# Set-up of an FFT mixing and ReGLU kernel: constant rows in the angle products, rows of x in fewer transfers, weights asked for in another order, batch 1 loaded behind a token and its mirror gathered

## The chip, the cores and the metric

The kernel runs on one core of a Trainium2 chip, in one launch. The core has TensorE (matrix products, accumulating in eight PSUM banks), VectorE, ScalarE, GpSimd and SyncE (SP), each with an instruction queue of its own that is worked off in order; DMAs are issued from the queues of SP, ScalarE and GpSimd. The metric is device time in microseconds (us), the median of the runs shown.

## The reference

x has 8 batches of 3008 rows with 256 channels, in float32. Its two-dimensional Fourier transform over rows and channels is taken, the real part kept, and each of the 24064 rows goes through a ReGLU layer with 1536 hidden units:

```python
X = np.fft.fft(x, axis=1)
X = np.fft.fft(X, axis=2)
a = X.real.astype(np.float32).reshape(8 * 3008, 256)
gate = np.maximum(a @ w_gate, 0.0)
val = a @ w_val
out = (gate * val @ w_out).astype(np.float32)
```

## The kernel before, in words

The transform over channels is folded into the weights: WA and WB are cosine and sine tables (TA, TB) times w_gate (index 0) or w_val (index 1), WM is WB scaled. The transform over rows is a product with cosine and sine tables (tabC, tabS) on folded rows. A real transform has mirror symmetry, so each batch is folded first: XD holds rows upward (`load_rows`, L91), XG the same rows mirrored, and their sums and differences, halved twice more over rows and channels, are kept as F and G in bfloat16, in three parts t of 128, 128 and 120 or 121 partitions. Row 0 of both halves has a place of its own (partition 120 of part 2). From F and G the DFT steps make U (cosine part) and V (sine part); CB is a row for channel 128, made by the nyquist step (L620) from FN, written to DRAM (`keep_nyquist`, L630) and read back on all partitions (`row_128`, L993).

Then for each of 12 slices of the hidden units a gate (U times WA plus V times WB, L774 and L775) and, by adding WM (L779), the gate of the mirrored rows; the same for the value; ScalarE's relu (L789), VectorE's product (L798), later in one step (L809). h times wo (L692) gives the output rows, evicted by ScalarE and stored from SP.

Order is written out by hand; each engine works in program order and only data dependencies are added. The stages:

- **Set-up** (0 to 21 us). GpSimd makes index vectors (`iota`, L216). TensorE spins on zeros (`spin`, L263). An angle product (`angle`, L301) is three matmuls into one bank: row index times column index (`urow`, `krow`, L304), plus a constant 3008 x 1024 (`stride`, `offset`, L305), minus 3008 times a rounded quotient (L306); ScalarE takes its sine and cosine into the odd half of the tables. `turn` (L337) reverses part 0 of the mirror on TensorE with a permutation matrix; parts 1 and 2 of the mirror are gathered with indirect DMAs from GpSimd's queue (`load_mirror`, L108). VectorE folds batch 0 (L392 to L410). `hold` (L105) writes one element per half of XD on GpSimd, so that the row load behind it, which covers these elements, waits until GpSimd has come that far: a token. `load_w` (L286) and L361 load the weights from GpSimd's queue. `dft_first` (L530) then makes the first U and V, for the odd columns, together with the first weights (`combine`, L555).
- **Even part of batch 0**, on GpSimd: L414 to L423 (behind `go`, which VectorE writes when its fold is done), then `even_turns` (L438).
- **Batch 1's rows** are asked for at L462 to L466. The mirror takes two steps: `reverse` (L126) copies rows in reversed order from DRAM to DRAM (xr), `reverse_0` (L132) puts row 0 into its place there, `load_reversed` (L136) brings XG in. All are on SP's queue.
- **Batch 0 in four blocks** of 376 or 377 columns, 12 tiles each. Block 0 uses `first_tile` (L856), which also carries the remaining weights and the even tables as extra steps; blocks 1 to 3 use `single_tile` (L839). `fold_steps(1)` (L174) is emitted at the start of block 2 and `fold_steps(2)` at the start of block 3, on GpSimd, each with the row loads of the next batch; the DFT steps of batch 1 follow the tiles of blocks 2 and 3, as many per tile as `DFT_0` (L743) says: row 0 of that table is for block 1, row 1 for block 2, row 2 for block 3. The 25 steps are the nyquist step, then 24 products; the CB load goes with product 6, row 0 of V (L996) with product 21.
- **Batches 1 to 7** run in a software pipeline (`slot`, L918) over blocks of 512, 512 and 481 columns.

Of the kernel before, what the change touches and what calls it, by code (L numbers as in the profile page):

```python
# [33 lines left out]
def kernel(  # L34
# [50 lines left out]
    nc.vector.memset(FN[:], 0.0)  # L85
# [5 lines left out]
    def load_rows(b, ts=range(3), queue=None):  # L91
        o = b * S * D
        for t in ts:
            for r in range(2):
                n = (128, 128, 120)[t]
                (queue if queue and r else nc.sync).dma_start(out=XD[0:n, r, t],
                                                              in_=dram(x, o + (1 + r * H + t * 256) * D, [[2 * D, n], [D, 2], [1, D]]))
            if t == 2:
                for r in range(2):
                    if b == 0:  # L100
                        nc.sync.dma_start(out=XD[121:128, r, t],
                                          in_=dram(x, o + (1 + r * H + t * 256 + 2 * 121) * D, [[2 * D, 7], [D, 2], [1, D]]))
                    nc.sync.dma_start(out=XD[120:121, r, 2], in_=dram(x, o + r * H * D, [[0, 1], [0, 2], [1, D]]))

    def hold(t):  # L105
        nc.gpsimd.memset(XD[0:1, :, t, 0, 0:1], 0.0)
# [6 lines left out]

    def load_mirror_0(b):
        for r in range(2):
            nc.sync.dma_start(out=XG[120:121, r, 2, :, :].rearrange("p a d -> p (a d)"),
                              in_=dram(x, b * S * D + r * H * D, [[0, 1], [1, 2 * D]]))
# [56 lines left out]
    def fold_steps(b):  # L174
# [13 lines left out]
        for t in range(3):  # L188
            for i in range(2):
                steps.append((1.1, lambda i=i, t=t: fold_pq(e, p, i, t)))  # L190
                if (t, i) == (1, 0) and b + 1 < B:
                    steps.append((0.0, lambda: load_rows(b + 1)))
# [19 lines left out]
    load_rows(0, (0,), nc.scalar)  # L212
    load_rows(0, (1,))

# [27 lines left out]
    urow = single("urow", [1, 6, 128], F16, pool=st_)  # L242
    krow = single("krow", [1, NJ], F16, pool=st_)
    stride = single("stride", [1, 128], F16, pool=st_)
    offset = single("offset", [1, NJ], F16, pool=st_)
# [10 lines left out]

    warm = single("warm", [128, 512], BF16, pool=st_)
    nc.vector.memset(warm[:], 0.0)
    nc.vector.memset(half_pi[:], PI / 2)
    nc.vector.memset(stride[:], float(S))  # L260
# [811 lines left out]
```

## Time and profile before

| what | us |
|---|---|
| runs | 645.42, 645.14, 639.0 |
| median of the runs | 645.14 |
| the profiled execution's own time | 638.55 |
| its span, first to last instruction | 636.8 |
| TensorE busy in the span | 624.5 |
| VectorE, ScalarE, GpSimd busy | 553.6, 449.7, 495.3 |

The profile is one execution. Busy time of TensorE counts matmuls in the pipeline, so it says that work was under way, not that TensorE ran at its peak. A line of a timeline has the start, the duration, the engine, the line of the kernel, the operation, the tiles written and read, the shapes, how many instructions were merged, and in brackets the idle time before it and what ended it. L96 is line 96 of the kernel.

More rows of the same execution that matter here, from its timeline and its waits:

| what | start, us | note |
|---|---|---|
| first gate of block 0 (L774) | 20.99 | the next matmul (L775) at 21.86 |
| GpSimd: fold of the even part (L419 to L423) | 17.98 | third part ends at 29.42 |
| GpSimd: even turns | 30.07 | end at 38.00 |
| wo asked for (L361) | 15.30 | 23.9 us to landing |
| first use of wo (L692) | 39.24 | |
| SP: reverse of batch 1 (L130) | 18.40 | issued by 21.00 |
| SP: reverse_0 of batch 1 (L134) | 33.31 | 8.00 for both, with the waits |
| SP: load_reversed of batch 1 (L139) | 41.54 | |
| the nyquist step (L620) | 74.44 | |

### The profile page before, as it was taken

The numbers are of one execution on the slowest core, as the hardware profiler recorded it, in microseconds if no ns is written. First come the engines' busy times: TensorE is split into PE (matmuls) and PEld (weight loads), VectorE is DVE, ScalarE is ACT, GpSimd is POOL, SyncE is SP. The second block draws the span as 40 slices with busy tenths as digits, with TensorE's granted clock in tenths as the row PEclk, the third lists the DMA queues.
The fourth block names the chain that finished last, engine by engine and source line by source line (L and its number), as shares of the span: only waits on it lengthen the run. The fifth ranks groups of instructions, "written<-read, shape, count | busy, mean of one in ns | idle before, by whom it ended". The sixth has DMA issues, their size and how long they took to land.

```text
span 636.8 us, 12502 instructions
## 1 busy us (share of the span) xinstructions
PE 624.5 (98%) x4105; PEld 400.1 (63%) x4152; DVE 553.6 (87%) x983; ACT 449.7 (71%) x813; POOL 495.3 (78%) x479
## 2 busy tenths in 40 slices
PE   9999999999999999999999999999999999999997
PEld 2456676566666666666666666666666666666666
DVE  8797566998999999988999899899899989999991
ACT  6786666777777677777777777777777777777752
POOL 8837683899899999798888989799896666666660
PEclk9999999999999999999999999999999999999999
DMA  8955845724273426414272424321211111211122
GB/s 253 227 129 166 208 155 156 179 85 147 65 180 110 140 75 145 146 45 141 62 201 91 139 69 105 81 59 43 76 51 47 43 59 54 55 38 51 52 58 84
DMA packets 65523, 67.96 MB, mean 107 GB/s; under 512 B 20067, under 2 KB 47267, under 8 KB 65458
## 3 DMA queue, kind: packets, MB, share of 16 engines
q1 hardware_dynamic: 61522, 63.14, 34.4%
q0 software_dynamic: 3504, 3.38, 2.9%
q8 instruction: 32, 0.52, 0.4%
q10 hardware_dynamic: 432, 0.66, 0.3%
q14 instruction: 33, 0.27, 0.1%
HBM read 43.41 MB, written 35.70 MB: 124 GB/s over the span
## 4 chain that ended last, share of the span: by engine, by line
PE 85%; DVE 5%; POOL 3%; DMA 3%; issue 2%; SPq 1%; ACT 1%; DVEq 0%; ACTq 0%; POOLq 0%
PE o L692 35%; PE v L775 10%; PE v L779 9%; PE g L904 8%; PE p L911 8%; PE v L774 7%; PE d L503 4%; DVE h L809 3%; DMA XD<-in_x_dram 1%; DMA XG<-in_x_dram,gidx 1%; DMA CB<-ch 1%; PE p L779 1%; DVE r L915 1%; PE d L620 1%; DVE h L798 1%
## 5 line engine op out<-in xcount | busy, mean ns | idle before, releaser
L916 POOL TENSOR_TENSOR r<-r 128x512 f32<-128x512 f32 (+1 forms) x252 | 314.6, 1253 | 98.1 <-DVE r L915 97.7
L809 DVE SCALAR_TENSOR_TENSOR h<-r,v 128x512 bf16<-128x512 f32 (+1 forms) x504 | 318.6, 674 | 40.0 <-PE v L779 27.2
L692 PE MATMUL o<-wo,h 128*128 128x256 bf16 x2172 | 329.5, 272 | 0.0
L692 PEld LDWEIGHTS <-h 128*128 128x128 bf16 x2220 | 216.9, 98 | 112.3 <-issue 2.1
L899 ACT ACTIVATE p<-CB,b 128x512 f32<-128x512 bf16 (+1 forms) x252 | 172.4, 684 | 73.8 <-DVE r L915 72.5
L907 ACT COPY r<-g 128x512 f32<-128x512 f32 (+1 forms) x252 | 145.6, 578 | 66.6 <-PE g L904 58.9
L915 DVE SCALAR_TENSOR_TENSOR r<-r,p 128x512 f32<-128x512 f32 (+1 forms) x252 | 169.0, 671 | 0.8 <-ACT r L907 0.8
L779 PE MATMUL v<-V,WM 128*128 128x512 bf16 (+3 forms) x296 | 108.5, 367 | 2.8 <-DVE h L809 1.6
L775 PE MATMUL v<-V,WB 128*128 128x512 bf16 (+3 forms) x296 | 108.6, 367 | 2.3
L904 PE MATMUL g<-V,WM 128*128 128x512 bf16 (+1 forms) x252 | 94.5, 375 | 0.4 <-ACT r L907 0.3
L911 PE MATMUL p<-U,WA 128*128 128x512 bf16 (+1 forms) x252 | 94.5, 375 | 0.0
L774 PE MATMUL v<-U,WA 128*128 128x512 bf16 (+3 forms) x252 | 91.9, 365 | 0.3 <-DVE h L798 0.3
L148 POOL TENSOR_TENSOR XG<-XG,XD 128x510 f32<-128x510 f32 x42 | 53.3, 1280 | 21.7 <-issue 14.2
L798 DVE TENSOR_TENSOR h<-r,v 128x376 bf16<-128x376 f32 (+1 forms) x88 | 44.7, 543 | 19.4 <-PE v L779 12.4
L774 PEld LDWEIGHTS <-WA 128*128 128x128 bf16 x348 | 33.9, 98 | 42.7 <-issue 13.9
L703 ACT COPY os<-o 128x512 f32<-128x512 f32 x92 | 52.6, 572 | 4.7 <-issue 4.5
L775 PEld LDWEIGHTS <-WB 128*128 128x128 bf16 x348 | 33.9, 98 | 34.7 <-issue 0.7
L789 ACT ACTIVATE r<-p 128x376 f32<-128x376 f32 (+1 forms) x80 | 38.5, 487 | 19.5 <-PE p L779 10.7
L156 POOL TENSOR_TENSOR AA<-XG 128x510 f32<-128x510 f32 x42 | 45.4, 1091 | 0.0
L779 PEld LDWEIGHTS <-WM 128*128 128x128 bf16 x348 | 34.0, 98 | 7.8 <-ACT WM L593 0.5
L904 PEld LDWEIGHTS <-WM 128*128 128x128 bf16 x252 | 24.7, 98 | 6.4 <-issue 1.0
L911 PEld LDWEIGHTS <-WA 128*128 128x128 bf16 x252 | 24.6, 98 | 3.4 <-issue 0.5
(174 smaller groups left out, 390.6 us busy)
## 6 DMA issues: line engine op xcount, KB each, us to landing
out_dram<-os SPq DMA_DIRECT2D x124, 128.0 KB
xr<-in_x_dram SPq DMA_DIRECT2D x14, 768.0 KB
XG<-xr SPq DMA_DIRECT2D x14, 768.0 KB
XD<-in_x_dram SPq DMA_DIRECT2D x31, 256.0 KB
out_dram<-os SPq DMA_DIRECT2D x35, 112.0 KB
XD<-in_x_dram SPq DMA_DIRECT2D x16, 240.0 KB
CB<-ch SPq DMA_DIRECT2D x7, 376.2 KB
out_dram<-os SPq DMA_DIRECT2D x13, 96.0 KB
```

The costliest lines, as they stand in the source:

```text
L148: e.tensor_tensor(XG[p, r, t, ::-1, 1:D], XG[p, r, t, ::-1, 1:D], XD[p, r, t, :, D - 1:0:-1], op=ALU.add)
L692: nc.tensor.matmul(st["p"][0:m, q, :], lhsT=lhs(f), rhs=wo[:, f, :], start=(f == 0), stop=(f == NF - 1))
L774: nc.tensor.matmul(bank[:, 0:st["n"]], lhsT=WA[i][:, st["f"]], rhs=st["us"], start=True, stop=False)
L775: nc.tensor.matmul(bank[:, 0:st["n"]], lhsT=WB[i][:, st["f"]], rhs=st["vs"], start=False, stop=True)
L779: nc.tensor.matmul(bank[:, 0:st["n"]], lhsT=WM[i][:, st["f"]], rhs=st["vs"], start=False, stop=True, skip_group_check=True)
L809: nc.vector.scalar_tensor_tensor(half_h(st, sign), in0=st["s"][1 + sign][:, 0:n], scalar=0.0, in1=st["v"][:, 0:n], op0=ALU.max, op1=ALU.mult)
L899: nc.scalar.activation(st["p"][:, 0:st["n"]], st["c"], ACTF.Copy, scale=b2[:, st["fi"]:st["fi"] + 1])
L904: nc.tensor.matmul(st["g"][:, 0:n], lhsT=WM[0][:, st["f"]], rhs=st["vs"], start=True, stop=True)
L907: nc.scalar.copy(q[:, 0:n], st["g"][:, 0:n])
L911: nc.tensor.matmul(st["p"][:, 0:n], lhsT=WA[0][:, st["f"]], rhs=st["us"], start=False, stop=True, skip_group_check=True)
L915: nc.vector.scalar_tensor_tensor(sp[:, 0:n], in0=q[:, 0:n], scalar=-0.5, in1=st["p"][:, 0:n], op0=ALU.mult, op1=ALU.add)
L916: nc.gpsimd.tensor_tensor(sm[:, 0:n], sp[:, 0:n], q[:, 0:n], op=ALU.add)
```

## The change

Five parts:

1. **Angle products.** `stride` and `offset` are dropped with their matmul. `urow` and `krow` get 95 partitions: partition 0 holds the indices as before, the other 94 are constant, 256 in one and 128 in the other, and 94 x 256 x 128 is 3008 x 1024. The constants are written as pairs of float16 through a float32 view. The memset of FN moves from the first instruction of VectorE to behind four quotients. One `spin` between the second angle and the first turn is dropped.
2. **Rows.** `load_rows` takes both halves in one DMA per part (three instead of six); row 0 and seven spare rows have functions of their own, issued early for batch 0. The first part of batch 0 still goes in two halves, from SP and ScalarE.
3. **Weights.** The first load of w_val moves ahead of the sign table and the products with it on GpSimd. In the first tile, the first weight step is placed between the two matmuls of the gate.
4. **Batch 1.** `hold` on all three parts, behind `go`, lets batch 1's rows start only then. `reverse(1)`, `reverse_0(1)` and `load_reversed(1)` are dropped; six gathers from GpSimd's queue, behind the even turns, bring the mirror. The mirror's row 0 is loaded from SP, ahead of `reverse(2)`.
5. **DFT steps of batch 1.** In block 2 they begin with tile 2 instead of tile 6, and in block 3 there are at most two per tile but for one of three.

```diff
-    def load_rows(b, ts=range(3), queue=None):
-        o = b * S * D
+    def load_rows(b, ts=range(3)):
         for t in ts:
-            for r in range(2):
-                n = (128, 128, 120)[t]
-                (queue if queue and r else nc.sync).dma_start(out=XD[0:n, r, t],
-                                                              in_=dram(x, o + (1 + r * H + t * 256) * D, [[2 * D, n], [D, 2], [1, D]]))
...
+            n = (128, 128, 120)[t]
+            nc.sync.dma_start(out=XD[0:n, :, t].rearrange("p r a d -> p r (a d)"),
+                              in_=dram(x, (b * S + 1 + t * 256) * D, [[2 * D, n], [H * D, 2], [1, 2 * D]]))
+
+    def load_row_0(b):
+        for r in range(2):
+            nc.sync.dma_start(out=XD[120:121, r, 2], in_=dram(x, (b * S + r * H) * D, [[0, 1], [0, 2], [1, D]]))
+
+    def load_mirror_0(b):
+        nc.sync.dma_start(out=XG[120:121, :, 2, :, :].rearrange("p r a d -> p r (a d)"), in_=dram(x, b * S * D, [[H * D, 2], [1, 2 * D]]))
+
+    def load_spare():
+        for X in (XD, XG):
+            nc.sync.dma_start(out=X[121:128, :, 2, :, :].rearrange("p r a d -> p r (a d)"),
+                              in_=dram(x, 512 * D, [[2 * D, 7], [H * D, 2], [1, 2 * D]]))
...
-    def hold(t):
-        nc.gpsimd.memset(XD[0:1, :, t, 0, 0:1], 0.0)
+    def hold(ts):
+        nc.gpsimd.memset(XD[0:1, :, ts, 0, 0:1], 0.0)
...
-    load_rows(0, (0,), nc.scalar)
+    for r in range(2):
+        load_half(0, r, (nc.sync, nc.scalar)[r])
     load_rows(0, (1,))
+    load_row_0(0)
+    load_mirror_0(0)
+    load_spare()
...
-    urow = single("urow", [1, 6, 128], F16, pool=st_)
-    krow = single("krow", [1, NJ], F16, pool=st_)
-    stride = single("stride", [1, 128], F16, pool=st_)
-    offset = single("offset", [1, NJ], F16, pool=st_)
+    KA, UC, KC = 95, 256.0, 128.0
+    urow = single("urow", [KA, 6, 128], F16, pool=st_)
+    krow = single("krow", [KA, NJ], F16, pool=st_)
...
     nc.vector.memset(warm[:], 0.0)
+    nc.vector.memset(krow[:].bitcast(F32), pair_of(KC))
+    nc.vector.memset(urow[:].rearrange("p c k -> p (c k)").bitcast(F32), pair_of(UC))
     nc.vector.memset(half_pi[:], PI / 2)
-    nc.vector.memset(stride[:], float(S))
-    nc.vector.memset(offset[:], OFF)
...
     load_w(0, 0)
     for r in range(2):
         load_mirror(0, 2, r)
+    load_w(1, 0)
     nc.gpsimd.memset(sgn[:], 1.0)
...
         nc.tensor.matmul(m[:, 0:NJ], lhsT=urow[:, c, :], rhs=krow[:], start=True, stop=False)
-        nc.tensor.matmul(m[:, 0:NJ], lhsT=stride[:], rhs=offset[:], start=False, stop=False)
         nc.tensor.matmul(m[:, 0:NJ], lhsT=minus[:], rhs=quot[c][:], start=False, stop=True)
...
     angle(1, 0)
-    spin(1)
     turn(0)
...
     nc.gpsimd.tensor_copy(go[:, 1:2], go[:, 0:1])
+    hold(slice(0, 3))
...
+    load_rows(1)
+    load_row_0(1)
+    load_mirror_0(1)
     for n, c in enumerate(even_order):
         even_turns(n, c)
-    load_rows(1)
-    reverse(1)
-    reverse_0(1)
-    load_reversed(1)
+    for n in range(6):
+        load_mirror(1, n // 2, n % 2)
     reverse(2)
...
-    DFT_0 = (0, 0, 0, 0, 0, 3, 0, 0, 4, 3, 3, 0), (0,) * 6 + (1,) * 6, (1, 3, 3, 3, 3, 3, 3, 0, 0, 0, 0, 0)
+    DFT_0 = (0, 0, 0, 0, 0, 3, 0, 0, 4, 3, 3, 0), (0, 0) + (1,) * 10, (2, 2, 2, 2, 2, 2, 3, 0, 0, 0, 0, 0)
...
         st["g"] = bank("g" if st["fi"] % 3 == 2 else "p")
-        two(st["g"], st, 0)
+        if st["fi"]:
+            two(st["g"], st, 0)
+        else:
+            nc.tensor.matmul(st["g"][:, 0:st["n"]], lhsT=WA[0][:, st["f"]], rhs=st["us"], start=True, stop=False)
+            extra.pop()()
+            nc.tensor.matmul(st["g"][:, 0:st["n"]], lhsT=WB[0][:, st["f"]], rhs=st["vs"], start=False, stop=True)
         relu(st)
```

## The prediction, before the changed kernel was run

> **What bounds the kernel now.** I read the page first, then the stages, then the order of time in the set-up and around the first batch border. Engine totals, then the shares of the chain:
>
> ```profile
> PE 624.5 (98%) x4105; PEld 400.1 (63%) x4152; DVE 553.6 (87%) x983; ACT 449.7 (71%) x813; POOL 495.3 (78%) x479
> ...
> PE 85%; DVE 5%; POOL 3%; DMA 3%; issue 2%; SPq 1%; ACT 1%; DVEq 0%; ACTq 0%; POOLq 0%
> ```
>
> TensorE carries the end. What the change can win is only what TensorE loses before its stream is dense, and that is in the first 20 us and around 105 us. The stages (span, busy us by engine, clock, DMA share, GB/s):
>
> ```profile
> 0.00:20.00 20.00, 18.64 (x67) 6.01 (x68) 15.47 (x47) 13.16 (x28) 16.73 (x37) 1.00 0.93 258
> ...
> 100.00:636.80 536.80, 528.25 (x3507) 344.49 (x3550) 479.29 (x817) 379.24 (x661) 421.71 (x370) 1.00 0.32 91
> ```
>
> 67 matmuls in 20 us against 6.5 per us later: the set-up is sparse although PE counts as busy. DMA is nearly full there (0.93). TensorE's set-up in order of time (start, duration):
>
> ```profile
> 2.71 0.49 PE L304 MATMUL g<-krow,urow 1*128 1x376 f16 x1
> 2.99 0.52 PE L305 MATMUL g<-offset,stride 1*128 1x376 f16 x1
> 3.44 0.49 PE L306 MATMUL g<-q,minus 128*128 128x376 f16 x1
> ...
> 4.89 0.63 PE L267 MATMUL o<-warm 128*128 128x512 bf16 x1
> ...
> 5.31 1.91 PE L339 MATMUL v<-XG,turned 128*128 128x512 f32 x2
> ...
> 9.66 0.33 PE L304 MATMUL d<-krow,urow 1*128 1x376 f16 x1
> 9.83 0.32 PE L305 MATMUL d<-offset,stride 1*128 1x376 f16 x1
> 10.08 0.33 PE L306 MATMUL d<-q,minus 128*128 128x376 f16 x1
> ```
>
> An angle takes three matmuls; the middle one costs 0.28 us start to start early and 0.17 later. From 9.66 to 20.99 (first gate matmul, L774) matmuls follow each other with no wait that the view names, so TensorE's own queue sets that stretch. Beside it, the chain of waits in order of time holds
>
> ```profile
> 9.05 5.60 DMA XG<-in_x_dram,gidx
> 14.73 1.23 DVE AA L396
> ```
>
> The last mirror of batch 0 lands at 14.65, just as VectorE (busy without a break from 9.76 to 17.70) reaches it. Last, the border to batch 1, from the timelines of GpSimd, the SP queue, ScalarE and TensorE:
>
> ```profile
> 52.20 7.92 POOL L148 TENSOR_TENSOR XG<-XG,XD 128x510 f32<-128x510 f32 x6 [14.20 <-issue]
> 81.90 7.38 POOL L148 TENSOR_TENSOR XG<-XG,XD 128x510 f32<-128x510 f32 x6 [7.53 <-DMA XG<-xr]
> 95.77 2.87 SPq L96 DMA_DIRECT2D XD<-in_x_dram  x6
> 100.04 0.40 SPq L993 DMA_DIRECT2D CB<-ch  x1
> 104.88 0.69 ACT L899 ACTIVATE p<-CB,b 128x512 f32<-128x512 bf16 x1 [1.14 <-DMA CB<-ch]
> 106.40 0.32 PE L779 MATMUL g<-V,WM 128*128 128x377 bf16 x1 [0.33 <-ACT r L789]
> ```
>
> The CB load stands on SP behind the rows of batch 3, which wait until GpSimd has folded batch 2 (begun when its reversed rows landed, 81.9). ScalarE waits 1.14 us for CB, and the relu queued behind that seed holds TensorE.
>
> **The change, part by part.** Sums go against the profiled execution: span 636.8, its own time 638.55, so 1.75 outside the span. The median of the runs shown, 645.14, lies 6.6 above it, the lowest, 639.0, 0.45 above.
>
> *Angles, spin.* Before turn(0) two L305 (0.28 each at least) and one spin (5.31 - 4.89 = 0.42) go: up to 0.98. The turn needs the mirror's first half, which the view gives no landing for; its weight load began at 4.89 with nothing named as the wait, so 0.42 is sure and 0.98 the upper end. I take 0.55, near the sure end, because SP's load was asked for only at 0.75-1.16 and the ones timed here take 4.7 us or more. angle(2,3) between the turns loses another L305 (7.45 to 7.90): 0.28 to 0.45, I take 0.30. The three later angles lose 0.17 each: 0.5. TensorE reaches L774 1.35 us sooner (bounds 0.9 to 1.9). The constants come as two memsets on 95 partitions (188 and 384 words); warm, 256 words, took 0.27, so about 0.2 and 0.4, against 0.17 + 0.37 for the two removed and 0.14 for FN, which moves behind four quotients. VectorE's first use of that time is unchanged within 0.2, and it is hidden behind GpSimd's iotas (krow 1.67, urow 2.07), which now wait for these memsets; without that cover it costs 0.2.
>
> *Cover.* VectorE follows turn(1), so its stretch to 17.70 moves 0.85 forward if the last mirror lands by 13.9. It should: the 256 KB of batch 1 issued at 10.64 now wait for the token behind VectorE's last read (about 17), and 256 KB at 258 GB/s is 1.0 us. If it does not move at all, VectorE still ends at 17.7, and TensorE's last part, from 18.67 - 1.35 = 17.3, first uses the last piece of it 1.15 us on (rows 18.67 to 19.82), at 18.5. So 0. Row transfers keep their 2 KB pieces and only halve SP's issues (0.4 us each, SP is not waited for before 95 us): 0. The gate weights' value half is asked for about 1.5 us sooner; combine(1) now needs it at 17.65 - 1.15 = 16.5, and the load takes 4.7 to 10.2 us from issue: 0 here, and without the move up to 1. The sign work on GpSimd slips 0.8 us (11.64 to 12.4), before combine(0) near 13.5.
>
> *First tile.* The weight step (0.43 on TensorE) enters the 0.55 us in which L775 waits for V, and its copy fills ScalarE's 0.90 idle before the first relu. VectorE paces block 0 (9.49 busy of 10 us from 30 to 40), so I take 0.2 of 0 to 0.43.
>
> *wo.* Asked for at 15.3, it lands 23.9 us later, at 39.2; its first use is at 39.24. All won so far would be lost here if it stayed. But the slow copy that runs beside it (reverse, SP 18.40) is dropped for batch 1, and batch 2's is queued behind the mirror of row 0, which waits for GpSimd's third fold (about 28.5). The six 256 KB loads ahead of it land within 10.2 us of issue; three times 256 KB at the median 6.9 would be 36 even one after the other. So 0, moved ahead of need.
>
> *Mirror of batch 1.* GpSimd ends the even turns at 38.00 - 0.85 = 37.2 and issues six gathers of about 1.07 + 0.30 (the four at 3.02 to 10.03): free at 45.4, where it was idle until 52.20. The fold's first G is complete 18.9 us after its start (71.10): 64.3 instead of 71.1. DFT steps now start four tiles sooner; the nyquist step moves from 74.44 to about 66, its FN is there at 54; the first sine step runs near 70. Slack 5.6 us: 0.
>
> *CB.* The CB step is now emitted in block 2, ahead of batch 3's rows on SP; it waits only for N and some outputs, some 15 us before its use. TensorE's gaps at 105.70 and 103.76 shrink: 0.7 (from 0.33, the named wait, to 1.14, ScalarE's). Row 0 of V stays behind those rows, at 102.22 before, and moves with the earlier fold. The DFT tables only redistribute matmuls: 0.
>
> Sum: 1.35 + 0.2 + 0.7 = 2.25. Span 634.55, time 636.3.
>
> **The rivals.** (1) *The tall runs come from elsewhere.* Two of three runs shown are 6 us above the profile. I think that the CB line explains them: reversed rows, fold, batch 3's rows, CB stand in series with no slack, so a copy late by some us passes to TensorE whole, and the change cuts this. No trace of such a run is here. If they have another source, the median keeps them: 645.14 - 2.25 = 642.9.
>
> (2) *wo or the mirror still sets the pace*: then the set-up's 1.55 is lost and CB's 0.7 stays: 637.9.
>
> (3) *TensorE gets its pace later.* The 376-column matmul goes every 0.28 us until 7.45 and every 0.17 from 9.66, with the clock row at 1.00 throughout; the change removes work that came before. If the pace comes 3 us later (a choice: under half of the 7 us from the first matmul), 3 us of matmuls at 0.28/0.17 add 1.9: 638.2. The Trainium skill (TensorE: Matmul & The Clock Gate, Part 1: The HAM clock gate) says that full rate follows about 3.4 us of sustained activity, in a window that runs free of the kernel; by that rule, with one window more, the loss would be an estimated 2.2 and the time 638.5. The trace agrees that a slow stretch comes first, not with its length.
>
> (4) *Slower: the gathers land late.* If they fare as wo did beside a slow copy (23.9 us from issue), the last lands at 37.2 + 23.9 = 61.1, then 2.6 us for its two folds and 11.1 for the rest (60.07 to 71.10): G at 74.8 against 69.9, a stall of 4.9, less 2.25: 641.2 against 638.55. It decides from a last landing at 56. Against it: the gathers at 7.69 and 9.05 took 6.8 and 5.6 with DMA full.
>
> **How the numbers follow.** Forecast 0.50, rival (1) 0.22, (2) 0.10, (3) 0.08, (4) 0.06, others 0.04. The time is the forecast's, 636.3. Its own range, with upper and lower ends summed (1.9 + 0.43 + 1.14 and 0.9 + 0 + 0.33), is 635.1 to 637.3; with 0.3% between executions, 633.2 to 639.2. The range runs on to (1): 633.3 to 643.3. One per cent, 6.4 us, is what a measurement here can tell. Against the median shown (645.14, limit 638.7) forecast, (2) and half of (3) are faster, 0.64; against runs like the profiled one they are the same. I weigh the first at two thirds: faster 0.43, same 0.52, slower 0.05 (others and the worst of (4)).
>
> **What would show it.** Right: L774 first near 19.6; two matmuls an angle; VectorE's t=2 fold near 13.9; wo landed before 36; GpSimd's batch 1 fold from 45 without a wait; no ScalarE wait for CB and TensorE dense from 101 to 106. Wrong: TensorE waiting on a G or FN between 62 and 75, slow matmuls after 9, first use of wo still at 39, or a span that moves by less than its start.

## The result, and the profile after

The changed kernel takes 645.02 us (median of 11 runs, 644.7 to 646.07), the kernel before 641.07 (11 runs, 639.0 to 645.42). The ratio is 1.0058, interval 1.0032 to 1.0083: slower by about half a per cent. 636.3 us was forecast, with a range of 633.3 to 643.3, and 645.0 lies above it. The profiled execution took 645.0, with a span of 643.2.

The totals by engine and the shares of the chain, from the page of the changed kernel:

```profile
PE 626.8 (97%) x4145; PEld 400.6 (62%) x4145; DVE 560.7 (87%) x983; ACT 449.9 (70%) x813; POOL 500.9 (78%) x486
...
PE 86%; POOL 5%; DVE 4%; issue 3%; ACT 1%; DMA 1%; DVEq 0%; POOLq 0%; ACTq 0%
```

DMA has shrunk in the chain (3% to 1%) and GpSimd has grown in it (3% to 5%). VectorE is busy 7.1 us longer with the same 983 instructions: not more work, but something in it that takes longer. The stages say where (columns as in the prediction):

```profile
0.00:20.00 20.00, 17.14 (x67) 6.37 (x68) 15.64 (x47) 14.14 (x30) 16.56 (x38) 1.00 1.00 231
20.00:40.00 20.00, 17.81 (x101) 9.39 (x100) 18.45 (x37) 17.56 (x40) 18.35 (x32) 1.00 0.72 178
40.00:60.00 20.00, 15.14 (x90) 9.22 (x90) 18.62 (x26) 10.53 (x24) 14.47 (x16) 0.83 0.36 115
60.00:100.00 40.00, 39.41 (x294) 26.67 (x293) 24.45 (x50) 24.52 (x54) 23.77 (x26) 1.00 0.54 146
100.00:643.20 543.20, 537.34 (x3599) 348.94 (x3596) 483.51 (x825) 383.10 (x669) 427.78 (x377) 1.00 0.33 92
```

The same stage of the kernel before:

```profile
40.00:60.00 20.00, 19.46 (x136) 12.68 (x135) 16.15 (x35) 15.35 (x34) 7.80 (x6) 1.00 0.62 169
```

Between 40 and 60 us TensorE runs 90 matmuls instead of 136, at a granted clock of 0.83 (0.99 or more until 52, then 0.50 to 58, in stretches of 2 us). VectorE runs 26 instructions instead of 35 and is called busier. Five places in the stream of both kernels pin it down:

| place | before, us | after, us | difference |
|---|---|---|---|
| first gate matmul of block 0 (L774, now L871) | 20.99 | 19.79 | -1.20 |
| first use of wo (L692, now L701) | 39.24 | 37.94 | -1.30 |
| gate_128, block 2 | 66.88 | 73.21 | +6.33 |
| first sine product of batch 1 | 108.02 | 114.11 | +6.09 |
| end of the span | 636.75 | 643.24 | +6.48 |

So the set-up gave nearly what was hoped for, and 7.6 us were lost between the first use of wo and gate_128, in block 1. VectorE there, after (timeline: start, duration):

```profile
45.02 0.31 DVE L460 TENSOR_SCALAR tabS<-tabS,wv 121x377 bf16<-121x377 bf16 x1
45.25 0.54 DVE L457 SCALAR_TENSOR_TENSOR AA<-AA 128x377 f32<-128x377 f32 x1
...
46.68 7.01 DVE L460 TENSOR_SCALAR tabC<-tabC,wv 121x377 bf16<-121x377 bf16 x1
53.61 0.60 DVE L455 SCALAR_TENSOR_TENSOR AA<-kvec,u,AA 128x377 f32<-128x377 f32 x1
```

Twin instructions of one size, the scales of even table 5: the one at 45.02 takes 0.31 us, the one at 46.68 takes 7.01. GpSimd in that time:

```profile
45.17 1.00 POOL L117 DMA_INDIRECT XG<-in_x_dram,gidx  x1 [0.30 <-issue]
46.20 7.37 POOL L150 TENSOR_TENSOR XG<-XG,XD 128x510 f32<-128x510 f32 x6
```

The six additions of batch 1's fold follow the last gather without a pause and end at 53.57; VectorE's instruction ends at 53.69. In what follows, an instruction "asks" at its start in the trace, and it is "held" for as long as it lasts beyond the time of an undisturbed twin. TensorE behind it:

```profile
53.74 0.47 PE L509 MATMUL d<-tabC,F 121*1 121x377 bf16 x1 [4.35 <-DVE tabC L460]
54.15 0.49 PE L783 MATMUL p<-U,WA 128*128 128x376 bf16 x1
54.43 0.52 PE L784 MATMUL p<-V,WB 128*128 128x376 bf16 x1
...
58.84 0.32 PE L784 MATMUL v<-V,WB 128*128 128x376 bf16 x1
```

It waits 4.35 us for the table that VectorE holds, and its matmuls then last 0.5 us instead of 0.32 until 58.84. In the profile of before the same fold (52.20, shown in the prediction) met only the last two table instructions, and VectorE was not held by it:

```profile
51.93 0.61 DVE L447 SCALAR_TENSOR_TENSOR AA<-kvec,u,AA 128x377 f32<-128x377 f32 x1
52.62 1.00 DVE L798 TENSOR_TENSOR h<-r,v 128x376 bf16<-128x376 f32 x2
53.54 0.55 DVE L449 SCALAR_TENSOR_TENSOR AA<-AA 128x377 f32<-128x377 f32 x1
```

There GpSimd paid: its first two additions, looked at one by one, took 1.47 and 1.59 us instead of 1.27. The change brought the fold 6.0 us forward, and the tables only 0.6 where nothing holds them (the last instruction of this form starts at 51.30 instead of 51.93 in the kernel with the fold behind the tables, below).

The Trainium skill (SBUF — State Buffer, Who interferes with whom) states a lock for this: VectorE and GpSimd share one pair of ports, a VectorE instruction with two inputs in memory, or one like a scale in its wide mode, contends with a GpSimd instruction that reads memory, and the later one blocks until the earlier is done. The traces agree that the two exclude each other, and that VectorE's products with one input in PSUM (L798, two in 1.00 us at 52.62 above) pass beside the fold. They do not agree with the length: 7.01 us is six GpSimd instructions and not one.

### The profile page after: what moved, and what is told of

Same layout as the page of the kernel before. It is cut to its first block, busy times and chain, and to the rows that moved or that the text cites. A ratio compares the mean times of both kernels' runs of the same rounds, so it can differ in the third digit from the quotient of the medians.

```text
span 643.2 us, 12518 instructions
## 1 busy us (share of the span) xinstructions
PE 626.8 (97%) x4145; PEld 400.6 (62%) x4145; DVE 560.7 (87%) x983; ACT 449.9 (70%) x813; POOL 500.9 (78%) x486
## 4 chain that ended last, share of the span: by engine, by line
PE 86%; POOL 5%; DVE 4%; issue 3%; ACT 1%; DMA 1%; DVEq 0%; POOLq 0%; ACTq 0%
PE o L701 35%; PE v L788 9%; PE v L783 8%; PE v L784 8%; PE g L918 8%; PE p L925 8%; PE d L512 4%; DVE h L818 3%; POOL XG L427 1%; POOL XG L150 1%; POOL XG L117 1%; DVE r L929 1%; PE p L788 1%; PE d L629 1%; PE p L784 1%
## 5 line engine op out<-in xcount | busy, mean ns | idle before, releaser
L701 PE MATMUL o<-wo,h 128*128 128x256 bf16 x2172 | 330.2, 273 | 0.0
L701 PEld LDWEIGHTS <-h 128*128 128x128 bf16 x2220 | 217.1, 98 | 112.4 <-issue 2.0
L783 PE MATMUL v<-U,WA 128*128 128x512 bf16 (+3 forms) x296 | 108.9, 368 | 0.3 <-DVE h L807 0.3
L798 ACT ACTIVATE r<-p 128x376 f32<-128x376 f32 (+1 forms) x80 | 38.5, 487 | 20.1 <-PE p L788 11.5
L158 POOL TENSOR_TENSOR AA<-XG 128x510 f32<-128x510 f32 x42 | 45.4, 1091 | 4.7 <-DVE AA L457 4.7
```

Source lines behind the costliest of these rows:

```text
L701: nc.tensor.matmul(st["p"][0:m, q, :], lhsT=lhs(f), rhs=wo[:, f, :], start=(f == 0), stop=(f == NF - 1))
L783: nc.tensor.matmul(bank[:, 0:st["n"]], lhsT=WA[i][:, st["f"]], rhs=st["us"], start=True, stop=False)
```

## The experiments

Three questions: is it the fold that holds VectorE; why for a whole run of additions; and is there a placing that keeps the gain. Where a median and a ratio are given, the kernel is compared with runs of the kernel before on the same chip (its medians there 640.2 to 640.7). Where a span alone is given, the kernel ran once, profiled.

### Which part of the change, and which VectorE instruction

Batch 1 as before, the set-up as changed:

```diff
-    hold(slice(0, 3))
...
-    load_mirror_0(1)
...
-    for n in range(6):
-        load_mirror(1, n // 2, n % 2)
+    reverse(1)
+    reverse_0(1)
+    load_reversed(1)
...
-    DFT_0 = ..., (0, 0) + (1,) * 10, (2, 2, 2, 2, 2, 2, 3, 0, 0, 0, 0, 0)
+    DFT_0 = ..., (0,) * 6 + (1,) * 6, (1, 3, 3, 3, 3, 3, 3, 0, 0, 0, 0, 0)
```

> The changed kernel with batch 1 loaded as in the kernel before (reversed in DRAM, no token behind go, the old table of DFT steps); the angle products, the row transfers, the weights' order and the first tile stay as changed. Theory (a): no collision, as GpSimd's folds start at 50 or later and the table's scaling ends near 46.5; first use of wo about 1.3 us sooner than in the kernel before, or held by wo at 39; the time 0.5 to 2 us below the kernel before. Theory (b), that the set-up edits themselves cost: 643 or more.

Measured: 639.57 us (639.0 to 640.78, 10 runs), ratio 0.9968 (0.9934 to 1.0002). The loss is gone, so it belongs to batch 1's part; the interval reaches 1, so a gain over the kernel before is not shown. But wo is late again; TensorE's waits:

```profile
PE o L700 <- DMA wo<-in_moe_w_out_dram: 1.4, 1, 1.4
PE g L568 <- DMA h<-in_moe_w_val_dram: 1.3, 1, 1.3
```

Its first use is at 41.20 instead of 37.94. In this kernel the set-up's 1.2 us are lost at wo, as the prediction's wo step feared if the mirrored copy stays; the token ahead of batch 1's rows was dropped with it, so which of the two delays wo is not told apart.

Table 5 scaled on ScalarE instead of VectorE:

```diff
-            steps += [lambda tab=tab: nc.vector.tensor_scalar(tab[r, 5, even_k], tab[r, 5, even_k], scalar1=wv[r], op0=ALU.mult, scalar2=None)
+            steps += [lambda tab=tab: act(tab[r, 5, even_k], tab[r, 5, even_k], ACTF.Copy, scale=wv[r])
```

> The changed kernel with one edit: the last step of the even table 5, tabS and tabC times wv in bfloat16, goes from VectorE to ScalarE. Theory (a): in the changed kernel VectorE's 7.01 us instruction at 46.68 (0.31 in the kernel before) is held off by GpSimd's six folds, which now start at 46.20 instead of 52.20; TensorE waits 4.35 us for it and then runs slowly until 58.6. Then here no VectorE instruction between 40 and 60 is above 1.5 us, TensorE has no wait for tabC above 0.5, the clock is 1.00 throughout, and the time is 6 to 7.6 us below the changed kernel's 645.0, so 637.4 to 639. Theory (b): the fold is only what GpSimd happens to do then, and the hold-up comes from the table's producer on ScalarE or from the gathers' traffic: then ScalarE's copy is late too and the time stays within 2 us of 645.

Measured: 645.11 us (643.65 to 648.2), ratio 1.0058 (1.002 to 1.0095). Theory (a) failed, and the time is that of theory (b). VectorE's next instruction with two inputs in memory is held in its place; its timeline:

```profile
49.16 4.95 DVE L455 SCALAR_TENSOR_TENSOR AA<-kvec,u,AA 128x377 f32<-128x377 f32 x1
```

It asked in the third addition and came free at 54.11, after the sixth had ended at 53.70. The victim changes, and the hold still ends with the sixth addition.

Table 5 made first, so that its scales run beside the gathers:

```diff
-    order, even_order = (1, 0, 3, 2, 5, 4), (1, 3, 5, 0, 2, 4)
+    order, even_order = (1, 0, 3, 2, 5, 4), (5, 1, 3, 0, 2, 4)
```

> The changed kernel with one edit in order alone: even table 5, the one that is scaled, is made first instead of third, so that its two tensor_scalar stand before the folds of batch 1 (near 40 us, GpSimd then issuing gathers, folds from 46). No engine's work changes. Theory (a): both tensor_scalar at or below 1 us, and a time within 1 us of the kernel with the scaling on ScalarE, 637.4 to 640. If the gathers hold VectorE as the folds do, they last 1 to 2 us and the time lies up to 2 us higher. Theory (b): 644 to 646.

Measured: 645.71 us (644.82 to 646.28), ratio 1.006 (1.0026 to 1.0095). The scales now take 0.38 and 0.31 us, as theory (a) had it, but the time is that of theory (b): L455, which now meets the fold, lasts 7.42 us. The gathers do not hold VectorE: the scale of 0.38 us overlaps one (that of 0.31 falls between two), and in the changed kernel L457 at 45.25 takes its usual 0.54 us inside the gather of 45.17 to 46.18.

One VectorE scale more, in the kernel before, put into its fold:

```diff
+    scratch = single("scratch", [128, NE], BF16)
+    nc.vector.memset(scratch[:], 1.0)
+    more.setdefault((1, 8), []).append(lambda: nc.vector.tensor_scalar(scratch[0:121], scratch[0:121], scalar1=wv[0:121], op0=ALU.mult, scalar2=None))
```

> The kernel before with one idle instruction more: a bfloat16 tensor_scalar on a scratch tile of 121x377 on VectorE in tile 8 of block 1 (near 54 us), while GpSimd folds batch 1 (52.2 to 60.1). Theory (a): it lasts until GpSimd's six folds are through, so about 5 to 6 us instead of 0.31, TensorE waits behind VectorE's products by 3 to 5 us, and the time is 4 to 7 us above the kernel before in the same rounds. Theory (b): it lasts 0.31 and the time does not move by 1 us. If VectorE is let in after the fold instruction that runs at that moment, it lasts at most 1.6 us.

Measured: the scale lasts 1.36 us, from 0.03 us into the third addition to its end; 641.19 us, ratio 0.9975 (0.9936 to 1.0015). Held, but for one addition only, which is the last of the three cases expected.

### The fold behind the tables

If the fold is the cause, the cure is to start it when VectorE has finished the tables. A GpSimd memset of a cell that the last table still reads does it (the tables' scratch AA and the fold's later steps share this memory); the products of batch 1 are dealt out later, to fit:

```diff
+        if b == 1:
+            steps.insert(0, (0.0, lambda: e.memset(spare[0:1, 6 * NE - 1:6 * NE], 0.0)))
...
-    DFT_0 = ..., (0, 0) + (1,) * 10, (2, 2, 2, 2, 2, 2, 3, 0, 0, 0, 0, 0)
+    DFT_0 = ..., (0,) * 4 + (1,) * 8, (2, 2, 2, 2, 3, 3, 3, 0, 0, 0, 0, 0)
```

> The changed kernel with two edits: one GpSimd memset of a cell that the last even table still reads is put ahead of batch 1's fold, so that the fold's first addition waits until VectorE has done the last of the even tables (about 52.8 us in place of 46.2), and the products of batch 1 are dealt out four tiles later into block 2, where F and G are now ready (about 72 us). Theory (the loss is VectorE held by GpSimd's run of six additions): no VectorE instruction of the tables lasts over 0.7 us, TensorE's waits of 4.35 us at L509 and the slow matmuls behind it are gone, the first use of wo stays at 37.9, the 1.2 to 1.3 us won in the set-up reach the end: span 635.5, time 637.4, range 636.3 to 639.0, faster than before's median and all runs within 2 us. Rival (the stretch from 38 to 67 us is slow for another reason, such as the transfers of the gathers or of batch 1's rows): block 1 keeps its loss, and the time stays at 643 or more. Second rival (batch 1 now comes too late for the products): TensorE waits for F or G in block 2, some 2 us, and the time is 639 to 641.

Measured: 638.41 us (638.09 to 638.78, 12 runs), ratio 0.9964 (0.9935 to 0.9993). GpSimd:

```profile
53.57 0.09 POOL L211 MEMSET AA<- 1x1 f32 x1 [7.25 <-DVE AA L459]
53.69 2.49 POOL L150 TENSOR_TENSOR XG<-XG,XD 128x510 f32<-128x510 f32 x2
```

GpSimd now stands still for 7.25 us, and the kernel is 6.6 us shorter than the changed one by the medians (645.02 - 638.41) and by the spans (643.2 - 636.6). No table instruction of VectorE lasts over 0.61 us, and the wait at L509 is gone. The second edit is not needed for it: the run behind the fifth table, below, has a memset alone and is 7.0 us shorter than the changed kernel, while a memset that makes no pause, further below, leaves the whole loss. That settles that the meeting with the fold is the cause. The 637.4 expected was too low by 1.0, though: gate_128 comes 0.64 us sooner than before, and of that 0.18 is left at the end (span 636.57 against 636.75). Where the rest goes was not followed up.

How much of the loss is the wait, and how much the slow matmuls behind it? The changed kernel with 20 matmuls put into the wait (their sums are read by nobody):

```diff
-                        part[2] = lambda par=par, mm=mm: (mm(par, 2), [mm(par, t, True) for t in range(3)])
+                        part[2] = lambda par=par, mm=mm: (mm(par, 2), [mm(par, t, True) for t in range(2)], fill(20 * par), mm(par, 2, True))
```

> The changed kernel with 20 matmuls of 512 columns put ahead of the last Nyquist product of block 1, on which TensorE waited 4.35 us; their sums go to a bank that is not read. Theory (the slow stretch from 53.7 to 58.6 us comes from TensorE having stood still): the product still waits for VectorE, until 53.7, but the matmuls behind it go at full pace, 376 columns in about 0.16 us instead of 0.31, and the end comes 2 to 2.5 us sooner, span 640.7 to 641.3. Rival (the slow stretch has another cause, such as the load of the other engines at that time): the matmuls behind the wait stay at 0.3 us and the span stays at 642.5 to 643.5.

```profile
49.38 4.49 PE L609 MATMUL o<-U,WA 128*128 128x512 bf16 x19
53.83 0.32 PE L509 MATMUL d<-tabC,F 121*1 121x377 bf16 x1
54.09 0.33 PE L789 MATMUL p<-U,WA 128*128 128x376 bf16 x1
```

That is TensorE's timeline. The matmuls behind keep 0.32 us, and the granted clock between 40 and 60 us is 1.00: the slow stretch came from standing still, as the theory said. Its price is 1.3 us (span 641.9 instead of 643.2, gate_128 at 71.93 instead of 73.21), not 2 to 2.5, since TensorE then catches up with VectorE and waits 0.69 for it. So of the 7.6 us, 4.35 are the named wait and 1.3 the slow pace; the other 2 are what is left over, perhaps the work that VectorE had lost and TensorE met later, which was not tried.

### One addition or the whole run

The same scale, asking 0.40 us into the fourth addition of the kernel before:

```diff
...
+    more.setdefault((1, 8), []).extend([lambda: nc.vector.memset(delay[:], 0.0)] * 3)
     more.setdefault((1, 8), []).append(lambda: nc.vector.tensor_scalar(scratch[0:121], ...))
```

> The kernel before with one further tensor_scalar of VectorE on scratch cells, as in the run where it was held 1.36 us, and three small memsets of VectorE ahead of it (cells that nothing reads), so that it asks some 0.4 us after the start of a GpSimd addition in place of 0.03 us. Theory A (it decides how late within a GpSimd instruction VectorE asks: past some tenths of a us the next GpSimd instruction is ahead of it in the queue, and so on at each border): it is held until the sixth addition ends, 4 to 5 us. Theory B (the long holds belong to folds that follow right on the gathers): it is let in at the end of the addition that runs, after at most 1.3 us.

Measured: the scale lasts 0.99 us, to the end of that addition. L447, which here asked 0.08 us into the first, lasted 1.59. Theory A falls.

The kernel with the fold behind the tables, and two scales that meet its fourth and fifth additions (`for fi in (9, 10)`, else as above):

> The changed kernel with batch 1's fold held behind the even tables (it starts at 53.7 us, some 7 us behind the last gather) and two further tensor_scalars of VectorE on scratch cells, in block 1's tenth and eleventh tile, when the fold's additions run. So far: VectorE was held 7.01, 4.95 and 7.42 us where the fold followed right on the gathers, and 1.36, 1.59 and 0.99 us in the kernel before, where GpSimd had stood idle ahead of it and the mirrored rows came by ordinary transfers. Theory B (what counts is that GpSimd goes from the gathers straight into the additions): here each scale lasts at most 1.4 us, and the span stays within 1 us of 636.6. Rival (what counts is that the additions read rows that gathers brought): the first scale is held to the end of the sixth addition, 3 us or more, and the span is 2 us longer or more.

Measured: 1.07 and 0.32 us, span 636.6. Gathered rows alone do not make the hold long.

The fold behind the fifth table instead of the sixth, so that it still meets the last two VectorE instructions:

```diff
...
+            steps.insert(0, (0.0, lambda: e.memset(spare[0:1, 5 * NE - 1:5 * NE], 0.0)))
```

> The changed kernel with the same GpSimd memset ahead of batch 1's fold, but on a cell of the fifth even table instead of the sixth: the fold starts at about 49.2 us, some 2.9 us behind the last gather, and VectorE's two instructions of the sixth table (about 51.3 and 52.9 us) still meet its additions. Theory B (straight from the gathers into the additions): each of the two is held at most 1.4 us, TensorE waits 2 us in all at most, span 636.5 to 639, time 638.3 to 641. Rival (additions on gathered rows hold VectorE to the end of their run however they begin): one of the two is held 4 us or more, until about 56.6, TensorE waits 3 us or more, time 641 to 644.

Measured: 638.01 us (637.76 to 638.6, 10 runs), ratio 0.9939 (0.99 to 0.9978), the best of the study. VectorE's two instructions that meet the fold:

```profile
51.29 0.91 DVE L457 SCALAR_TENSOR_TENSOR AA<-kvec,u,AA 128x377 f32<-128x377 f32 x1
...
53.03 0.70 DVE L459 SCALAR_TENSOR_TENSOR AA<-AA 128x377 f32<-128x377 f32 x1
```

They last 0.31 and 0.16 us longer than alone. It looked as if a pause of GpSimd decided. Three runs tried that. Twelve scratch additions between the gathers and the fold:

```diff
...
+    for _ in range(12):
+        nc.gpsimd.tensor_tensor(delay[:], delay[:], delay[:], op=ALU.add)
```

> The changed kernel with twelve further additions of GpSimd on scratch cells (128x128 each, by size some 0.3 to 0.4 us) between the last gather and batch 1's fold, which so starts at about 50 us with GpSimd never idle since the gathers, long after the gathers' packets have landed (49.0 us at the latest so far). Theory I (what counts is that GpSimd has not been idle since the gathers): a VectorE instruction with two inputs in SBUF, or a scale, that asks from 46.3 on is held over many GpSimd instructions, 3 us or more. Theory T (what counts is the time since the gathers, some 3 us): what asks before about 49 us is held over several, what asks after it over one only, at most 1.4 us.

and 40 of them in the kernel before, with no gathers at all:

> The kernel before (batch 1 by the mirrored copy, no gathers since 10 us) with 40 additions of GpSimd on scratch cells (128x128 each) right behind the rounding of the even tables, from about 38 us on without a gap. VectorE's table instructions from 38 to 52 us meet them. Theory G (the long holds need gathers just ahead): each VectorE instruction is held for one addition at most, 0.4 us, and none lasts over 1.1 us. Rival (any run of additions without a gap holds VectorE to its end): the first table instruction that asks is held several us.

In both, each scratch addition waits for the one before, and a pause of 0.08 us stands between them. VectorE was held some 0.2 us beyond its own time in either (the longest lasted 0.78 and 0.81 us). As a test of idle time against gathers they failed, since GpSimd did pause; what they show is that such pauses let VectorE in. The span of the first is 637.5, that of the second 644.3, which has another cause, told below.

A memset in between, with no pause (the cell was free before the last gather):

```diff
...
+            steps.insert(0, (0.0, lambda: e.memset(spare[0:1, 4 * NE - 1:4 * NE], 0.0)))
```

> The changed kernel with the same memset of one cell between the last gather and batch 1's fold, but on a cell of the fourth even table, which VectorE has read at 45.9 us, before the last gather has been issued (46.2): one more short instruction and no gap. Theory (the gap counts, not the instruction): VectorE is held to the end of the sixth addition as in the changed kernel, 4 us or more, span 641 to 645. Rival (the instruction between is enough): held at most 1.4 us, span 636 to 638.

Measured: VectorE's scale lasts 7.06 us, span 643.0. The instruction between changes nothing.

A copy that waits for table 5's cosines:

```diff
...
+            steps.insert(0, (0.0, lambda: e.tensor_copy(spare[0:1, 4 * NE - 1:4 * NE], tabC[0:1, 5, 0:1])))
```

> The changed kernel with one GpSimd copy of a cell ahead of batch 1's fold that waits for VectorE's scaling of table 5's cosines (end at about 47.1 us): the fold starts at 47.3 us, some 0.9 us behind the last gather's instruction and ahead of the landing of its last packets (49.0 us). Theory (a gap in which GpSimd stands still is enough): each VectorE instruction that meets the fold (48.5 and 51.3 us) is held for one addition at most, 1.4 us; span 636 to 637.5. Rival (the time since the gathers counts, 2.9 us and more were short, 0 us long): the one at 48.5 us is held until the sixth addition ends at about 54.7, 5 us or more, and the span is 641 or more.

Measured: 647.09 us (646.82 to 647.64), ratio 1.011 (1.0094 to 1.0127). The cosines came 2 us later here (a relu of ScalarE stood 2.30 us for a reason that the view does not give, and TensorE 1.92 behind it), so the pause was 3.28 us, longer than the 2.87 behind the fifth table. Still, in the timeline of all engines:

```profile
49.42 0.42 POOL L211 CAST AA<-tabC 1x1 f32<-1x1 bf16 x1 [3.28 <-ACT r L800]
...
50.67 6.95 DVE L459 SCALAR_TENSOR_TENSOR AA<-AA 128x377 f32<-128x377 f32 x1
```

VectorE asks 0.86 us into the first addition and is held to the end of the sixth, a pause of 3.28 us notwithstanding. So a pause ahead of the fold is not what decides.

Pauses inside the fold, which again follows right on the gathers:

```diff
+        if b == 1:
+            for k in range(6, 0, -1):
+                cell = lambda r=(k - 1) % 2, t=(k - 1) // 2: e.tensor_copy(spare[0:1, 8 * NE + 2 * t + r:8 * NE + 2 * t + r + 1], XG[0:1, r, t, 1, 1:2])
+                steps.insert(k, (0.0, cell))
```

> The changed kernel with a GpSimd copy of one cell behind each of the six additions of batch 1's fold, which reads what the addition has just written: GpSimd waits for its own result there, 0.08 us by the run with scratch additions, in which VectorE went in at each such pause. The fold follows the gathers without a gap (46.2 us) and ends some 1.5 us later. Theory (a pause between two GpSimd instructions lets VectorE in): no VectorE instruction is held over 1.4 us; TensorE's waits at L509 under 1.5 us; span 636 to 638. Rival (only what lies between the gathers and the fold counts): table 5's scale is held through the run as in the changed kernel, 7 us, span 642 or more.

Measured: no table instruction lasts over 1.57 us, span 638.9; 640.64 us (639.49 to 642.27), ratio 1.0003 (0.998 to 1.0026). The fold starts at 46.31, as in the changed kernel, and most of the loss is gone: it is the long hold that costs, and not the early fold by itself. The span misses the 636 to 638 expected. TensorE waits 3.9 us in all between 36 and 70 us, against 1.7 with the fold behind the sixth table; 1.8 of it falls at 46.5 and 48.3, about a pause of ScalarE of 1.59 us that had begun before the fold. Such a pause stands also in the copy's kernel (the 2.30 us) and in that with the scale on ScalarE (1.86 us); what causes it is open, and the times of these three hold its price.

Last, a scale that asks 0.88 us into the first addition, with the fold behind the sixth table (`for fi in (8,)`):

> The changed kernel with the fold held behind the sixth table (start at 53.7 us, 7 us behind the gathers) and one further scale of VectorE on scratch cells in block 1's ninth tile, which asks at about 54.6 us, 0.9 us into the first addition. Seen so far: in four of the five long holds VectorE asked during the first addition, in one during the third; the short ones began in the first (0.08 us into it), the second, third and fourth. Theory P (asking during the first addition, away from its start, gives the long hold): it lasts 5 us or more, until the sixth addition ends at about 61.1. Theory T (the long hold belongs to the 4.5 us behind the gathers, within which all five began): it lasts at most 0.8 us.

Measured: 0.51 us, span 636.6. Theory P falls. What there is, with the end of the last gather's instruction as zero:

| kernel | VectorE asks, us behind the last gather | in addition | lasts, us |
|---|---|---|---|
| changed | 0.5 | 1st | 7.01 |
| filled wait | 0.5 | 1st | 7.04 |
| memset between | 0.5 | 1st | 7.06 |
| table 5 first | 0.4 | 1st | 7.42 |
| scale on ScalarE | 2.9 | 3rd | 4.95 |
| copy of a cosine between | 4.5 | 1st | 6.95 |
| behind the fifth table | 5.0, 6.7 | 2nd, 3rd | 0.91, 0.70 |
| behind the sixth, scales | 8.3, 11.4 | 1st, 4th | 0.51, 1.07 |
| kernel before with one scale more, no gathers near | - | 1st, 3rd, 4th | 1.59, 1.36, 0.99 |

All long holds began within 4.5 us of the gathers, all short ones of an unbroken run of additions 5.0 us or more behind them or with no gathers near. That fits a rule of time, but 4.5 and 5.0 are close, and the copy at 4.5 differs in more than time. Why VectorE is passed over at up to five borders between additions stays open.

### Where the runs above 643 us come from

Of 113 runs of the kernel before, 23 took over 643 us. The theory that it loses the same collision in them:

> The kernel before with the same GpSimd memset ahead of batch 1's fold, and nothing else. In the profile of before the first two additions met the last two instructions of the tables and let them in first, by 0.3 us. Theory (the wide spread of the kernel before, 638 to 647.6, is the same collision, lost in those executions in which batch 1's rows land some tenths of a us sooner): with the fold behind the tables no run is above 641.5, the median is 638.5 to 639.5. Rival (the spread comes from elsewhere): the median stays at 640 to 641 and single runs above 643 remain.

Measured, with the same memset ahead of its fold: 640.52 us (639.03 to 647.77, 12 runs), ratio 0.9999 (0.9965 to 1.0033). The theory falls; the spread has another source. Its own profile (span 639.9) points to one: matmuls with 376 columns last 0.5 us until 14 us instead of 9.7. The extreme is the run with 40 scratch additions (span 644.3). TensorE's groups between 9.9 and 20 us there (count, busy us, mean ns of one):

```profile
L542 PE MATMUL o<-tabS,G 128*128 128x376 bf16 x4 | 2.0, 493 | 0.0
```

and of the profiled execution of before:

```profile
L538 PE MATMUL o<-tabS,G 128*128 128x376 bf16 x8 | 2.3, 331 | 0.0
```

In the former the full pace comes only after 20 us, and combine(0) is at 18.55 instead of 14.64, long before the first scratch addition (39.55); the first use of wo follows at 44.65 instead of 39.24, 5.4 of the 7.5 us by which its span is longer than that of the profiled before. No run of the kernel before itself above 643 us was profiled. The clock row of both says 1.00, so this is read from the mean time alone. Two kernels split the set-up. The constant rows alone, in the kernel before:

```diff
+    KA, UC, KC = 95, 256.0, 128.0
...
-    krow = single("krow", [1, NJ], F16, pool=st_)
+    krow = single("krow", [KA, NJ], F16, pool=st_)
...
-        nc.tensor.matmul(m[:, 0:NJ], lhsT=stride[:], rhs=offset[:], start=False, stop=False)
```

> The kernel before with the constant rows in the angle products alone (95 rows, two products per angle instead of three); transfers, the warm-up matmul and batch 1 as before. Seen so far: of four profiles of kernels with the old set-up one had TensorE at the slow pace until 14.1 us instead of 9.7, ended 3 us later, and single runs of these kernels reach 642 to 648, while kernels with the new set-up stay within 2.2 us (but for the one in which table 5 is scaled on ScalarE). Theory (the products with one row decide when the clock is granted): median 638.5 to 639.5, no run above 641.5. Rival (the transfers of the set-up decide it): the spread of before stays, median 640 to 641, single runs above 642.

and the changed transfers with the angle products as before:

> The complement: the changed kernel's set-up transfers (wider rows, weights asked for sooner, the order of the queues) with three products per angle and the warm-up matmul as before, and batch 1 by the mirrored copy as before. Theory (the products with one row decide when the clock is granted): the spread stays, median 640 or more, single runs above 642. Rival (the transfers decide it): median 639 to 640 and all runs within 2.2 us.

Measured: constant rows alone 640.99 (639.07 to 642.39, 12 runs), ratio 0.9993 (0.9962 to 1.0024), none above 643; transfers alone 640.02 (638.72 to 645.36, 12 runs), ratio 0.999 (0.9958 to 1.0022), two above 643. In the first the theory's numbers fail: its median is not below 639.5 and three runs lie above 641.5, one of them at 642.39, as the rival had it. In the second the theory's hold. Counted afterwards over the study, kernels with one-row products and no scratch additions have 27 of 146 runs above 643, those with 95 rows and no long hold none of 57. In the 14 profiles with 95 rows the full pace comes between 6.2 and 10.3 us, in the six with one row at 9.5 to 10 four times, at 14 and after 20. So by this count the long runs go with the products of one row. By themselves the two kernels are too few for it (none of 12 against two of 12 above 643), and the mechanism was not tried. The median is not won by constant rows alone; in their profile TensorE waits 3.0 us for the gate weights and 2.2 for wo.

## Why the prediction was wrong

- *Angles and spin*: right. 1.35 us forecast for the first gate matmul, 1.20 measured, with two products per angle. TensorE's set-up, after:

```profile
2.47 0.50 PE L313 MATMUL g<-krow,urow 95*128 95x376 f16 x1
2.92 0.50 PE L314 MATMUL g<-q,minus 128*128 128x376 f16 x1
...
4.58 2.05 PE L348 MATMUL v<-XG,turned 128*128 128x512 f32 x2 [0.55 <-DMA XG<-in_x_dram]
...
8.17 0.32 PE L313 MATMUL d<-krow,urow 95*128 95x376 f16 x1
...
13.44 0.38 PE L569 MATMUL v<-h,TA 128*128 128x512 bf16 x1 [1.12 <-DMA h<-in_moe_w_gate_dram]
```

  The turn moved 0.73 (0.55 taken) and now waits for its load; the gate weights hold combine(0) by 1.12.
- *Cover*: right in what it costs, wrong in the time. VectorE's t=2 fold comes at 15.07, not 13.9, since the mirror still landed at 14.99 (14.65 before).
- *First tile, wo*: right for wo, which landed at 30.9 instead of 39.2, and its first use moved with the rest, to 37.94. The first tile brought 0.10 us (-1.30 against -1.20), not 0.2.
- *Mirror of batch 1, "Slack 5.6 us: 0"*: this step failed, and decides the result. The fold did start without a wait at 46.2 (45.4 forecast), the gathers had landed by 49, and TensorE waited for no G. The first G was complete at 69.67, though, and not at 64.3: the fold's next step (L158) stood 4.72 us for the last table instruction of VectorE, which the hold had made late. The step failed because I costed the earlier fold by its inputs and its consumers and did not look at what VectorE runs at the new time. Five of VectorE's table instructions start between 46.2 and 53.5 us where nothing holds them, four with two inputs in memory and one scale. The fold moved from the end of the tables into their middle: 7.6 us, where 0 stood.
- *CB*: the mechanism was right, the size not. ScalarE no longer waits for CB, but the border gains 0.24 us (+6.33 to +6.09), not 0.7.
- *Rivals*: none was this one. (4), gathers landing late, had the right place (batch 1's mirror) and sign with the wrong mechanism. (3) did not come: the pace was there at 8.17. (1) said that the long runs of before have another source than the CB line, to which I had laid them. Two profiles above, neither of them of the kernel before itself, are late from the set-up on, long before CB; that the median then keeps these runs did not come true (none of 57 with 95 rows and no long hold).
- *The sum*: even without the hold the forecast was too low. With the fold behind a table the spans are 636.2 and 636.6, not 634.55; of the 2.25 us summed up, 0.2 to 0.6 reach the end.

## What to carry to other kernels

When a change moves an engine's block of work earlier, list what the other engines run at the new time, not only what the block waits for and who waits for it: here VectorE and GpSimd held each other, and the idle gap on GpSimd had kept the fold clear of VectorE's tables. An instruction that lasts twenty times its twin's time, with an unbroken run of GpSimd work beside it, is the sign. A memset of a cell that the victim still reads puts the run behind it for 0.09 us of GpSimd, where GpSimd has time to wait. And take a median over runs as the base of a sum only once it is known what the runs differ in.

## What the runs showed of the hardware

- A VectorE instruction that meets a run of GpSimd additions may be held to the end of the addition that runs (it then lasted 0.5 to 1.6 us) or to the end of the whole run (4.95 to 7.42 us, six additions of 1.25 us). In the three kernels with a pause of some 0.08 us between GpSimd's instructions it was let in each time.
- Gathers issued by GpSimd (about 1.0 us each) did not hold VectorE: L457 took its usual 0.54 us inside one, and a scale that overlapped one 0.38 us instead of 0.31.
- TensorE's full pace came 8 us after the span's start in one profile (95 rows) and after 20 us in another (one row), with matmuls under way by the profile from 1.2 and 1.3 us on. The Trainium skill (TensorE: Matmul & The Clock Gate, Part 1: The HAM clock gate) gives some 3.4 us of sustained activity; the run with 20 us does not agree, unless matmuls with one row do not count as activity, which was not tried by itself. After a wait of 4.35 us the slow pace lasted until 58.84, 5.1 us from the first matmul; the direction agrees, and filling the wait took it away.
